# Interleaving the first-half depth of two batches at the start of a second layer, in two PSUM banks

## The chip, the cores and the metric

One core of a Trainium2 chip. The metric is the device time of one execution in microseconds (us); the median of several executions is quoted with the lowest and the highest. Where two kernels are compared, their executions alternate on the same chip. The spans of the profile are about 1.7 us shorter than the device time of the same execution.

An execution is labelled slow when it is over 1.5% above the fastest of the same kernel.

## The reference

A gated linear attention (four batches, eight heads of 48, sequence 768) is followed by a two-layer perceptron on its 3072 token vectors of 384:

```python
def _moe_ref(x, w_in, w_out):
    h = x @ w_in                          # 3072 x 384 by 384 x 2048
    g = h * (1.0 / (1.0 + np.exp(-h)))    # Silu
    return (g @ w_out)                    # by 2048 x 384
```

The attention runs over the sequence in six chunks of 128 tokens; the perceptron runs over the same chunks, four batches of 128 tokens each.

## The kernel before

The order of the program is the order on each engine. The perceptron's matmuls are "fillers": small closures in a list, which `fill(n)` emits between the steps of the attention, so that TensorE (PE) always has something to do. One part of the second layer is four matmuls of 128x128 by 128x384; a batch of a chunk takes four parts (sixteen depth tiles `ft`), all summed in one PSUM bank.

```python
opss = {}

def l2(sc, b, part):                      # second layer, chunk sc, batch b
    if part == 0:
        opss[0] = ps.tile([128, HD], FP, name="ops", tag="moe", bufs=3)
    ops = opss[0]
    for ft in range(4 * part, 4 * part + 4):
        nc.tensor.matmul(ops, gts[sc][:, ft, b * C:(b + 1) * C], wout[:, ft, :],
                         start=(ft == 0), stop=(ft == NFT - 1))
    if part == 3:
        osb = wrk.tile([128, HD], FP, name="osb", bufs=4)
        nc.vector.tensor_copy(out=osb, in_=ops)
        tt = b * S + sc * C
        nc.sync.dma_start(out=out[tt:tt + C, :], in_=osb)

def l2s(sc, b0=0, b1=B):
    return [(1.0, lambda b=b, part=part: l2(sc, b, part))
            for b in range(b0, b1) for part in range(4)]
```

The three banks of the ring "moe" are shared by these accumulators and by the first layer's tiles (`hps`), which ScalarE (ACT) empties through Silu. VectorE (DVE) copies the finished accumulators out (`osb`).

The second layer's weights come in two halves through GpSimd's (POOL's) own queue, depth tiles 0 to 7 and 8 to 15:

```python
def wout_part(g):
    nc.gpsimd.dma_start(
        out=wout[:, 8 * g:8 * g + 8, :],
        in_=moe_w_out[1024 * g:1024 * g + 1024, :].rearrange("(f p) n -> p f n", p=128))
```

They are issued between elementwise operations of POOL, and the second layer of chunk 0 begins soon after (short lines joined, cuts marked):

```python
wout_part(0)
sums(1); state(1)
...
wout_part(1)
fill(1)
sums(a); state(a)
...                                       # units 5 and 6 of the attention start
fillers.extend(l1s(1, 0, 2) + l2s(0))     # then chunk 0's second layer
sums(b_); state(b_)
fill(.5)
half_state(0); half_state(2)
front(B + 2)                              # POOL: ku, rku_f, kc of unit 6
```

## Time and profile before

| | |
|---|---|
| time, median of the first three executions | 197.36 us (197.13 to 197.82) |
| span of the profiled execution, which took 196.87 us | 195.2 us |
| PE busy | 97% |
| first matmul of the second layer | 46.60 us |
| ninth, the first that needs the second weight half | 49.54 us |
| second weight half issued / landed | 37.13 us / about 48.9 us |

A line of a timeline has the start in us, the duration, the engine, the line of the program, the operation, what it writes and reads, the shape and the count of merged instructions; brackets tell idle time just before it and what ended it. A line of busy time by stretch has the window, its length, then the busy time of PE, PE's weight loads, DVE, ACT and POOL, with the number of instructions of each, and last the granted PE clock, the DMA share and GB/s.

### The profile page before, as it was taken

How to read it: one execution, taken by the hardware profiler on the slowest of the kernel's cores; microseconds unless marked ns; L12 is line 12 of the kernel's file. 1: busy time of each engine (PE TensorE's matmuls, PEld its weight loads, DVE VectorE, ACT ScalarE, POOL GpSimd, SP SyncE). 2: the span in 40 equal slices, each digit the busy share in tenths (PEclk: the TensorE clock that was granted, in tenths of full speed). 3: DMA queues.
4: the chain of work that ended last, by engine and by line, in shares of the span. 5: the costliest groups of instructions: out<-in, count | busy, mean ns of one | idle time of the engine just before them, and what ended most of it. 6: DMA issues, size and time to landing. Idle time of an engine off the chain costs nothing.

```text
span 195.2 us, 4922 instructions
## 1 busy us (share of the span) xinstructions
PE 188.3 (97%) x1916; PEld 126.5 (65%) x1916; DVE 115.6 (59%) x233; ACT 91.0 (47%) x207; POOL 115.1 (59%) x145
## 2 busy tenths in 40 slices
PE   7989999899999999999999999999999999999993
PEld 2757778788667787665657656557656556644563
DVE  6985757884866775885477677457566344210121
ACT  3385587798212543226771025692026680069300
POOL 4679979989975779669668837844537710000000
PEclk9999999999999999999999999999999999999999
DMA  4999999999894674385646486615651011310022
GB/s 77 225 196 153 187 233 191 162 187 194 170 230 124 142 172 100 105 183 112 124 96 121 119 182 146 141 34 118 142 140 44 20 22 44 99 43 0 3 82 81
DMA packets 89696, 24.12 MB, mean 124 GB/s; under 512 B 82888, under 2 KB 89672, under 8 KB 89672
## 3 DMA queue, kind: packets, MB, share of 16 engines
q1 hardware_dynamic: 85980, 20.65, 48.9%
q0 software_dynamic: 3680, 3.15, 11.0%
q8 instruction: 15, 0.25, 0.5%
q14 instruction: 9, 0.07, 0.1%
q10 hardware_dynamic: 12, 0.00, 0.0%
HBM read 20.45 MB, written 4.72 MB: 129 GB/s over the span
## 4 chain that ended last, share of the span: by engine, by line
PE 80%; POOL 11%; DVE 2%; DMA 2%; issue 2%; SPq 1%; ACT 0%; POOLq 0%
PE ops L374 31%; PE hps L362 27%; PE ae L271 10%; PE xs L246 4%; POOL kc L197 3%; POOL rku_f L192 2%; POOL ku L186 2%; DMA kin<-in_k_dram 2%; PE y L297 2%; POOL vu L209 2%; PE y L294 2%; PE sps L313 1%; PE ops L388 1%; DVE am L280 1%; POOL win L417 1%
## 5 line engine op out<-in xcount | busy, mean ns | idle before, releaser
L365 ACT ACTIVATE gT<-hps 128x256 f16<-128x256 f32 (+1 forms) x128 | 59.7, 493 | 51.2 <-PE hps L362 49.5
L362 PE MATMUL hps<-xT,win 128*128 128x256 f16 (+1 forms) x384 | 69.2, 326 | 0.2
L374 PE MATMUL ops<-wout,gT 128*128 128x384 f16 x368 | 63.8, 326 | 0.0
L362 PEld LDWEIGHTS <-win 128*128 128x128 f16 x384 | 35.3, 98 | 23.2 <-issue 0.8
L374 PEld LDWEIGHTS <-gT 128*128 128x128 f16 x368 | 34.7, 98 | 22.4
L280 DVE TENSOR_TENSOR am<-ae,maskM 128x512 f16<-128x512 f32 x24 | 16.6, 692 | 30.6 <-PE ao L273 30.6
L378 DVE COPY osb<-ops 128x384 f32<-128x384 f32 x23 | 12.8, 555 | 28.8 <-PE ops L374 28.7
L209 POOL TENSOR_TENSOR vu<-vin,rku 128x384 f32<-128x384 f32 x23 | 19.0, 828 | 15.2 <-DVE rku L203 15.1
L271 PEld LDWEIGHTS ae<-rk 48*128 48x128 f32 x192 | 23.1, 187 | 7.4 <-issue 4.8
L271 PE MATMUL ae<-rk 48*128 48x128 f32 x192 | 27.6, 285 | 0.2 <-DVE rk L234 0.2
L273 PE MATMUL ao<-rk 48*128 48x128 f32 x192 | 27.6, 285 | 0.0
L186 POOL TENSOR_TENSOR ku<-kin,u_bc 128x384 f32<-128x384 f32 x24 | 24.1, 1006 | 5.0 <-ACT u_bc L153 3.6
L263 ACT CAST rT<-rk 112x512 f16<-112x512 f32 x20 | 12.3, 615 | 30.9 <-DVE rk L257 30.9
L257 DVE TENSOR_TENSOR rk<-xs,pif 112x512 f32<-112x512 f32 x40 | 25.6, 682 | 1.7 <-PE xs L246 1.7
L192 POOL TENSOR_TENSOR rku_f<-rin,ku 128x384 f32<-128x384 f32 x24 | 24.1, 1005 | 1.9
L197 POOL TENSOR_TENSOR kc<-kin,lamC 128x384 f16<-128x384 f32 x24 | 24.0, 1001 | 0.0
L273 PEld LDWEIGHTS ao<-rk 48*128 48x128 f32 x192 | 23.1, 187 | 0.0
L304 DVE TENSOR_TENSOR y<-y,vu 128x384 f16<-128x384 f32 x24 | 13.4, 557 | 8.9 <-POOL vu L209 3.6
L327 POOL CAST stb<-st 112x384 f16<-112x384 f32 x12 | 6.0, 503 | 20.7 <-DVE st L322 20.7
L280 DVE TENSOR_TENSOR am<-ao,maskM 128x512 f16<-128x512 f32 x24 | 16.4, 681 | 0.0
L203 DVE TENSOR_REDUCE rku<-rku_f 128x8 f32<-128x384 f32 x24 | 13.2, 550 | 2.4 <-POOL rku_f L192 2.0
L329 POOL TENSOR_TENSOR sdec<-st,pif 112x384 f32<-112x384 f32 x16 | 13.3, 835 | 0.9 <-ACT gT L365 0.8
(72 smaller groups left out, 167.1 us busy)
## 6 DMA issues: line engine op xcount, KB each, us to landing
rin<-in_r_dram SPq DMA_DIRECT2D x24, 192.0 KB, 2.9
kin<-in_k_dram SPq DMA_DIRECT2D x24, 192.0 KB, 3.5
vin<-in_v_dram SPq DMA_DIRECT2D x24, 192.0 KB, 3.6
out_dram<-osb SPq DMA_DIRECT2D x23, 192.0 KB, 1.9
win<-in_moe_w_in_dram POOLq DMA_DIRECT2D x4, 384.0 KB, 6.2
wout<-in_moe_w_out_dram POOLq DMA_DIRECT2D x2, 768.0 KB, 10.8
xT<-y SPq DMA_TRANSPOSE x18, 2.3
out_dram<-osh SPq DMA_DIRECT2D x1, 128.0 KB, 1.7
```

What stands on the lines that cost most here:

```text
L186: nc.gpsimd.tensor_tensor(out=L["ku"], in0=kin[i % NIN][:, :, 0:D], in1=u_bc, op=ALU.mult)
L192: nc.gpsimd.tensor_tensor(out=L["rku_f"], in0=rin[i % NIN][:, :, 0:D], in1=L["ku"], op=ALU.mult)
L197: nc.gpsimd.tensor_tensor(out=kc[i % NKC][:, :, 0:D], in0=kin[n][:, :, 0:D], in1=lamC, op=ALU.mult)
L209: nc.gpsimd.tensor_tensor(out=L["vu"], in0=vin[i % NIN], in1=L["rku"].unsqueeze(2).broadcast_to([128, H, D]), op=ALU.mult)
L257: nc.vector.tensor_tensor(out=rk[:, :, :, 64 * g:64 * g + 64], in0=xs[g][0:PR], in1=lam(g), op=ALU.mult)
L271: nc.tensor.matmul(ae[:, p, :], L["kT"][0:D, p, :], L["rT"][0:D, p, :], start=True, stop=True)
L273: nc.tensor.matmul(ao[:, p, :], L["kT"][64:PR, p, :], L["rT"][64:PR, p, :], start=True, stop=True)
L280: nc.vector.tensor_tensor(out=am, in0=a, in1=maskM.unsqueeze(1).broadcast_to([128, NP, C]), op=ALU.mult)
L304: nc.vector.tensor_tensor(out=L["y16"], in0=L["y"], in1=L["vu"], op=ALU.add)
L362: nc.tensor.matmul(hps, win[:, q, ft * 128:(ft + 1) * 128], xts[sc][:, q, b0:b1, :].rearrange("p b t -> p (b t)"), start=(q == 0), stop=(q ...
L365: nc.scalar.activation(out=gts[sc][:, ft, b0 * C:b1 * C], in_=hps, func=AF.Silu)
L374: nc.tensor.matmul(ops, gts[sc][:, ft, b * C:(b + 1) * C], wout[:, ft, :], start=(ft == 0), stop=(ft == NFT - 1))
```

## The change

The intent: begin the second layer with work that needs only the first half of the weights. The accumulator is now kept per batch, and the list of parts of chunk 0 is reordered, so that two batches run their first eight depth tiles before either needs the other half.

```diff
     def l2(sc, b, part):
         if part == 0:
-            opss[0] = ps.tile([128, HD], FP, name="ops", tag="moe", bufs=3)
-        ops = opss[0]
+            opss[b] = ps.tile([128, HD], FP, name="ops", tag="moe", bufs=3)
+        ops = opss[b]
...
-    fillers.extend(l1s(1, 0, 2) + l2s(0))
+    f = l2s(0)
+    fillers.extend(l1s(1, 0, 2) + f[0:2] + f[4:6] + f[2:4] + f[6:])
```

## The prediction

> **What bounds the kernel now.** I read the page first: its table of busy time, the strip of forty slices, and the chain of work that ended last.
>
> ```profile
> PE 188.3 (97%) x1916; PEld 126.5 (65%) x1916; DVE 115.6 (59%) x233; ACT 91.0 (47%) x207; POOL 115.1 (59%) x145
> PE   7989999899999999999999999999999999999993
> PE 80%; POOL 11%; DVE 2%; DMA 2%; issue 2%; SPq 1%; ACT 0%; POOLq 0%
> ```
>
> TensorE (PE) is busy for 97% of the span and carries 80% of the chain. The other engines appear in the chain early: listed in order of time, it is PE work almost without a break from about 38.8 us to 192.2 us, with nothing but PE from 46.76 to 61.57 us. The change lies in exactly that stretch: it reorders the start of chunk 0's second layer (the "ops" matmuls, L374), which begins at 46.6 us.
>
> The intent is easy to see from the code. The second-layer weight is loaded in two halves by GpSimd's queue (L421), depth tiles 0 to 7 and then 8 to 15. Before, batch 0 runs through all sixteen tiles at once, so its ninth matmul needs the second half. After, the first eight tiles of batch 1 come in between. The change therefore helps only if that ninth matmul waits for the transfer. I looked for such a wait in three views. First the PE timeline, with start, duration and group:
>
> ```profile
> 46.60 1.46 PE L374 MATMUL ops<-wout,gT 128*128 128x384 f16 x8
> ...
> 49.21 0.39 PE L246 MATMUL xs<-ident,kin 64*112 64x64 f32 x8
> 49.54 2.12 PE L374 MATMUL ops<-wout,gT 128*128 128x384 f16 x12
> ...
> 52.05 3.41 PE L374 MATMUL ops<-wout,gT 128*128 128x384 f16 x20
> ...
> 56.61 0.40 PE L246 MATMUL xs<-ident,kin 64*112 64x64 f32 x8
> 56.94 2.12 PE L374 MATMUL ops<-wout,gT 128*128 128x384 f16 x12
> ```
>
> The ninth matmul is the first of the x12 group at 49.54 us. It follows the kin transposes at 49.21 by 0.33 us. One unit later the same pair stands at 56.61 and 56.94, again 0.33 us apart, and there no transfer is in question. So the ninth matmul started when its turn came. Because matmul ends are modelled in the page, this comparison of starts is better evidence than the busy share.
>
> Second, the busy time by stretch (window, its length, PE busy with count, then the other engines):
>
> ```profile
> 46.60:49.60 3.00, 3.00 (x43) 2.23 (x41) 1.55 (x4) 2.29 (x6) 2.92 (x4) 1.00 1.03 185
> 49.60:52.00 2.40, 2.40 (x28) 1.62 (x28) 2.40 (x5) 0.27 (x2) 2.32 (x4) 1.00 0.76 152
> 52.00:55.40 3.40, 3.40 (x27) 1.92 (x24) 2.42 (x6) 1.30 (x3) 2.36 (x3) 1.00 1.10 245
> 55.40:61.40 6.00, 6.00 (x73) 4.38 (x73) 4.12 (x8) 0.62 (x1) 4.26 (x6) 1.00 0.71 169
> ```
>
> PE's busy time equals the length of every stretch; its clock is 1.00. There is no hole to close. Third, the transfer itself: queue q0 carries these weights, and its share of the DMA engines in the half microsecond up to 48.5 us and the next one is
>
> ```profile
> q0 software_dynamic: 20, 0.01, 16.1%
> q0 software_dynamic: 1, 0.00, 0.1%
> ```
>
> Its last packet falls just after 48.5 us. The second transfer was issued at 37.13 us and took 11.8 us to land: 37.13 + 11.8 = about 48.9 us. The ninth matmul starts at 49.54, so the data were there 0.6 us early.
>
> **What the Trainium skill says.** "TensorE: Matmul & The Clock Gate", Part 2, the step-by-step, says that only weight loads are pulled ahead and that the matmuls "stay in program order". A late weight half would hold all PE work behind it, and giving PE another batch to do first is the right cure. The 0.33 us pitch agrees that nothing was held here. "DMA: Bandwidth & Descriptors", on why a DMA increments its semaphore by 16, says that only the full count means that all data has landed; so it is the last packet that counts, and I took the landing at 48.9 us, not the bulk of the packets before 47.5. "PSUM — Partial Sum Buffer", the four PSUM rules, says that two accumulation groups open at once in the same bank and quadrant cannot both begin with the flag that starts a group. That is why the two batches need two banks, and the change gives them that; the trace of before, where one group is open at a time, cannot show it.
>
> **The change part by part.** It adds and removes no arithmetic: all 64 second-layer matmuls of chunk 0, each 128x384, remain, and the instruction order on PE, read from the compiled programs, has the same 2586 rows. Only the accumulator and depth tiles of the groups change.
>
> The second layer runs in parts of four matmuls, named here by batch and part. Before: 0-0, 0-1, 0-2, 0-3, 1-0, 1-1, 1-2, 1-3. After: 0-0, 0-1, 1-0, 1-1, 0-2, 0-3, 1-2, 1-3. A part takes 4 x 0.1625 = 0.65 us, since the chain has eight ops matmuls in 1.30 us (46.76 to 48.06). The first need for the second weight half moves back by two parts, 1.30 us, from 49.54 to about 50.84 us. Slack grows from 0.6 to about 1.9 us. **Worth on the path in this profile: 0.** If an execution has the transfer later by d, the gain is max(0, min(d - 0.6, 1.3)) us; at most 1.3 us or 0.66% of 197.36.
>
> The new costs, each against its slack:
> - Batch 1's accumulator is opened two parts sooner, at 49.54 instead of 50.84 us. It takes the bank of the fifth of the six first-layer tiles just before, whose Silu is in a pair that runs on ScalarE (ACT) from 47.35 for 0.66 us. Free by 48.0: no wait.
> - Batch 0's accumulator closes later. Part 0-3 is the first 0.65 us of the x20 group, so it ends about 52.8 us. Batch 3 next needs that bank at about 58.3 us. The order on VectorE (DVE) changes with it: the copy of batch 0, before at 51.59 us, comes after y and state, as the compiled order shows. DVE lines before:
>
> ```profile
> 51.59 0.55 DVE L378 COPY osb<-ops 128x384 f32<-128x384 f32 x1
> 52.15 0.56 DVE L304 TENSOR_TENSOR y<-y,vu 128x384 f16<-128x384 f32 x1
> 52.62 0.73 DVE L322 TENSOR_TENSOR st<-sps,sdec 48x192 f32<-48x192 f32 x2
> 54.20 0.56 DVE L378 COPY osb<-ops 128x384 f32<-128x384 f32 x1 [0.85 <-PE ops L374]
> ```
>
> y can start perhaps 0.1 us earlier, the state ends near 53.25, batch 0's copy runs 53.3 to 53.85, in the 0.85 us hole, and batch 1's copy stays at 54.20. Batch 0's bank is thus free 4.4 us early. Cost 0.
> - On the SP queue the store of batch 0 precedes the transpose of y and three loads. The store moves from 52.43 to about 53.9 us, the transpose from 53.20 to about 54.6, so landing (2.3 us, DMA issue list) near 57. The first-layer matmuls that read this half of xT start at 61.41 us. Cost 0. The loads move by the same 1.4 us, and feed a unit several 7 us units away.
>
> Sum: 0 removed, 0 added, and -0.2 us that I allow for executions in which the weights come late: the profiled run took 196.87 us and the three timed ones 197.13 to 197.82, so a late transfer may be among the causes of that spread, though nothing shows it.
>
> **The rivals.** (1) The wait is real in timed executions and hidden in the profiled one. For: the slack is only 0.6 us of an 11.8 us transfer, which shares the engines with q1. Against: the spread of the times is under 0.7 us. It would give 196.1 to 197.0 us. (2) A new wait: two accumulators held at once out of three rotating banks starve the first layer, or DVE's later copy delays y. For: the ring has three banks. Against: no first-layer tile is opened between 46.6 and 61.4 us, and the slacks above are 1.5 us and more. It would give 198 us. (3) The delayed SP queue collides with later loads or the transpose, and PE waits once. Against: 4 us of slack. If one wait of 1 us arose, 198.4 us.
>
> **Range and chances.** The main course is 197.36 - 0.2 = 197.2 us. Low end 196.5: most of rival 1. High end 197.9: the top of the times before. Two per cent is 3.9 us, three times the most that the reorder could save and more than any of the rivals costs. So faster 0.01, same 0.98, slower 0.01.
>
> **What would show it.** In the changed kernel's profile the x8, x12 and x20 groups should start at the same times relative to each other; the matmul that follows the kin transposes by 0.33 us should now write batch 1's accumulator; two osb copies should stand back to back on DVE behind the state; the transpose of y should issue 1.4 us later; PE's busy time in these stretches should still fill them. The prediction would be wrong if the time fell by over 0.7 us (timed runs hide a wait), or if a wait for Silu, an osb copy or xT appeared ahead of a matmul.

## The result and the profile after

| kernel | median us | range | executions |
|---|---|---|---|
| before | 197.36 | 197.13 to 197.82 | 6 |
| changed | 197.28 | 196.81 to 197.73 | 6 |

The ratio is 0.9993 with a 95% interval of 0.9974 to 1.0013: the same. Ratios here are the mean time of one kernel's fast executions over that of the other's from the same rounds, so not quite the ratio of the medians quoted beside them.

The page of the changed kernel, its busy times, the strip of PE and the shares of the chain that ended last:

```profile
PE 189.3 (97%) x1916; PEld 127.5 (65%) x1916; DVE 115.7 (59%) x233; ACT 91.0 (46%) x207; POOL 115.0 (59%) x145
PE   7989999899999999999999999999999999999993
PE 82%; POOL 9%; DVE 5%; issue 2%; ACT 0%; POOLq 0%; DVEq 0%
```

PE is as full as before. Its timeline, for the groups that the prediction showed:

```profile
47.45 1.46 PE L374 MATMUL ops<-wout,gT 128*128 128x384 f16 x8
...
50.06 0.39 PE L246 MATMUL xs<-ident,kin 64*112 64x64 f32 x8
50.39 2.12 PE L374 MATMUL ops<-wout,gT 128*128 128x384 f16 x12
...
52.90 3.41 PE L374 MATMUL ops<-wout,gT 128*128 128x384 f16 x20
...
57.47 0.39 PE L246 MATMUL xs<-ident,kin 64*112 64x64 f32 x8
57.79 2.12 PE L374 MATMUL ops<-wout,gT 128*128 128x384 f16 x12
```

Count each start from the first matmul of the second layer. Before, the groups came 2.94, 5.45 and 10.34 us after it (49.54, 52.05 and 56.94 less 46.60). After, they come 2.94, 5.45 and 10.34 us after it (50.39, 52.90 and 57.79 less 47.45). The reordered matmuls keep the same pace to the hundredth of a us. From that first matmul to the end of the span it is 195.2 - 46.60 = 148.60 us before and 196.0 - 47.45 = 148.55 us after (spans are given to 0.1 us). Two of the stretches, moved by the 0.85 us, show PE without a hole and at full clock, as before:

```profile
47.45:50.45 3.00, 3.00 (x43) 2.22 (x41) 1.55 (x4) 1.80 (x5) 2.92 (x4) 1.00 0.99 181
50.45:52.85 2.40, 2.40 (x28) 1.62 (x28) 2.07 (x4) 0.75 (x2) 2.32 (x4) 1.00 0.70 142
```

The 0.85 us by which this profiled execution is behind arises long before the change. The first group of first-layer matmuls already starts at 16.40 us, 0.84 us later than the 15.56 us of before. The PE timeline shows two filler matmuls and the group after them, first in the kernel before:

```profile
4.76 0.60 PE L127 MATMUL spin<-junk 128*128 128x512 f16 x2
5.20 0.55 PE L151 MATMUL rows<-ident,cols_sb 112*128 112x112 f32 x4
```

and the same in the changed kernel:

```profile
4.84 1.03 PE L127 MATMUL spin<-junk 128*128 128x512 f16 x2
5.66 0.95 PE L151 MATMUL rows<-ident,cols_sb 112*128 112x112 f32 x4
```

Here the fillers took 1.03 us instead of 0.60 us and the group after them 0.95 us instead of 0.55 us, and the next group started at 6.41 us instead of 5.58 us. These instructions are the same in both kernels. Three later profiles (t_now, the changed kernel again, and t_late below) start their first layer at 15.83, 16.01 and 15.64 us; so this is spread between executions. It also means that 197.73 us, the slowest of the changed kernel's six executions, owes its excess to its start and not to a wait for the weights.

What did move is DVE's order. Its timeline after:

```profile
53.00 0.56 DVE L304 TENSOR_TENSOR y<-y,vu 128x384 f16<-128x384 f32 x1 [0.48 <-PE y L297]
53.48 0.73 DVE L322 TENSOR_TENSOR st<-sps,sdec 48x192 f32<-48x192 f32 x2
54.24 0.56 DVE L378 COPY osb<-ops 128x384 f32<-128x384 f32 x1
55.05 0.56 DVE L378 COPY osb<-ops 128x384 f32<-128x384 f32 x1 [0.26 <-PE ops L374]
```

Batch 0's copy now stands behind y and the state, in a hole that was there. The SP queue's timeline, with the store of batch 0 and the transpose of y, before:

```profile
52.43 0.68 SPq L380 DMA_DIRECT2D out_dram<-osb  x1
53.20 1.22 SPq L344 DMA_TRANSPOSE xT<-y  x1
```

and after:

```profile
54.83 0.36 SPq L380 DMA_DIRECT2D out_dram<-osb  x1
55.24 1.21 SPq L344 DMA_TRANSPOSE xT<-y  x1
```

Counted from the first second-layer matmul the transpose went from 6.60 to 7.79 us, 1.19 us later, and nothing on PE waited for it.

### The profile page after: what moved, and what is told of

Same layout as the page of the kernel before. It is cut to its first block, busy times and chain, and to the rows that moved or that the text cites. A ratio compares the mean times of both kernels' runs of the same rounds, so it can differ in the third digit from the quotient of the medians.

```text
span 196.0 us, 4920 instructions
## 1 busy us (share of the span) xinstructions
PE 189.3 (97%) x1916; PEld 127.5 (65%) x1916; DVE 115.7 (59%) x233; ACT 91.0 (46%) x207; POOL 115.0 (59%) x145
## 4 chain that ended last, share of the span: by engine, by line
PE 82%; POOL 9%; DVE 5%; issue 2%; ACT 0%; POOLq 0%; DVEq 0%
PE ops L374 31%; PE hps L362 27%; PE ae L271 10%; PE xs L246 4%; POOL kc L197 2%; PE spin L127 2%; PE y L297 2%; POOL ku L186 2%; DVE am L280 2%; PE y L294 2%; POOL rku_f L192 2%; POOL vu L209 1%; PE sps L313 1%; PE ops L388 1%; POOL win L417 1%
## 5 line engine op out<-in xcount | busy, mean ns | idle before, releaser
L365 ACT ACTIVATE gT<-hps 128x256 f16<-128x256 f32 (+1 forms) x128 | 59.7, 493 | 51.0 <-PE hps L362 49.3
```

What stands on the lines that cost most here:

```text
L365: nc.scalar.activation(out=gts[sc][:, ft, b0 * C:b1 * C], in_=hps, func=AF.Silu)
```

## The experiments

The theory: in the kernel before, no matmul waits for the second weight half, so the reorder has nothing to remove; it buys 1.30 us of tolerance per two parts moved. The rivals: the timed executions hide a wait which the profiled one does not show; or the reorder has a gain that is eaten by a cost in banks, copies or the queue. If the theory holds, a transfer made late on purpose must make the kernel before wait and the changed one wait less.

In a sentence on the names: "b" is the order before, "a" the changed order, "t" an order in which three batches come first.

### The weights late by several us

In three kernels the second half is issued after POOL's elementwise work for unit 6, the third unit of chunk 1:

```diff
-    wout_part(1)
...
     front(B + 2)
+    wout_part(1)
```

Kernel b_late is the order before with this edit.

> The kernel before, with the second half of the second-layer weights issued later on GpSimd: after the elementwise work for unit 6, at about 44.4 us instead of 37.1 us. Estimate of the landing: the second transfer before lay behind the first in the same queue (first landed at 43.5, second at 48.9, so 5.4 us of moving), and the first needed about 2 us from issue to its first packets; so 44.4 + 2.2 + 5.5 = about 52.1 us. My theory (nothing waited in before, slack 0.6 us; the reorder is worth whatever the transfer is later than that, up to 1.3 us): PE now stands about 52.1 - 49.5 = 2.6 us ahead of the ninth ops matmul, and the time is 197.4 + 2.6 = about 200.0 us (199.0 to 201.0). Rival (timed runs of before already waited for this half, by some tenths of a us): the time grows by the full delay of 3.2 us, to about 200.6 us. Rival (the transfer is hidden anyway and its place does not matter): 197.4 us.

Kernel a_late is the changed order with it.

> The changed kernel with the same later issue. My theory: the first need is two parts (1.30 us) later, so of the 2.6 us stall that the kernel before has, 1.3 us remain, ahead of the seventeenth ops matmul; time about 198.7 us, that is 1.3 us (0.65%) below b_late. Rival (two open accumulators or the moved copies cost something that hides the gain): difference to b_late under 0.7 us. Rival (the transfer's place does not matter): equal to b_late and to the kernel before.

Kernel t_late has it too, and takes the reorder one batch further, so that all three banks are open:

```diff
-    fillers.extend(l1s(1, 0, 2) + f[0:2] + f[4:6] + f[2:4] + f[6:])
+    fillers.extend(l1s(1, 0, 2) + f[0:2] + f[4:6] + f[8:10] + f[2:4] + f[6:8] + f[10:])
```

> The same later issue, and three batches run the first half of their depth before any runs the second, so all three banks of the ring are open at once. The first need then comes after six parts, at about 52.7 us in the profile of before, so a landing at 52.1 us leaves no stall: time about 197.3 us, 1.3 us below a_late. Rival (three open accumulators starve the ring): a new wait of PE for a copy by VectorE or a Silu, and a time above a_late's.

Six executions of each, with the kernel before beside them at 197.45 us (196.99 to 198.44, 11 executions):

| kernel | median us | range | executions at clock below 0.995 | ratio of fast executions to before |
|---|---|---|---|---|
| b_late | 202.21 | 199.25 to 204.87 | 4 of 6 | 1.0149 |
| a_late | 199.56 | 198.06 to 201.62 | 2 of 6 | 1.0069 |
| t_late | 197.13 | 196.86 to 198.74 | none of 6 | 0.9999 |

The executions of b_late were 203.84 (the profiled one), 202.41, 199.25, 204.87, 202.01 and 200.20 us, with mean clocks of 0.983, 0.991, 0.999, 0.983, 0.991 and 0.998. Those of a_late were 199.42 (profiled), 198.97, 198.06, 199.70, 201.62 and 201.21 us, with 1.000, 1.000, 0.999, 1.000, 0.991 and 0.991. So the profile of b_late is of an execution labelled slow, and what follows for its clock is read from that profile.

The PE timeline of b_late around its ninth second-layer matmul:

```profile
47.52 1.46 PE L374 MATMUL ops<-wout,gT 128*128 128x384 f16 x8
...
53.76 4.00 PE L374 MATMUL ops<-wout,gT 128*128 128x384 f16 x12 [3.23 <-DMA wout<-in_moe_w_out_dram]
...
58.52 3.89 PE L374 MATMUL ops<-wout,gT 128*128 128x384 f16 x20
...
63.88 2.12 PE L374 MATMUL ops<-wout,gT 128*128 128x384 f16 x12
```

and of a_late, where the twelve are split by the wait:

```profile
46.99 1.46 PE L374 MATMUL ops<-wout,gT 128*128 128x384 f16 x8
...
49.93 1.47 PE L374 MATMUL ops<-wout,gT 128*128 128x384 f16 x8
53.39 0.81 PE L374 MATMUL ops<-wout,gT 128*128 128x384 f16 x4 [1.99 <-DMA wout<-in_moe_w_out_dram]
```

and of t_late, where the group of twenty runs through:

```profile
52.36 3.41 PE L374 MATMUL ops<-wout,gT 128*128 128x384 f16 x20
```

This is the wait that the change is meant for. With the order before it is 3.23 us. With the changed order eight more matmuls go first and 1.99 us are left, 1.24 us less. These are two executions, so count again from the first second-layer matmul: the data came at 6.24 us in b_late (53.76 - 47.52) and at 6.40 us in a_late (53.39 - 46.99), and PE ran dry at 3.01 and at 4.41 us. The need moved by 1.40 us by these modelled ends, where the prediction's arithmetic from starts said 1.30. With three batches first no wait is left: in the profiled t_late the data landed at 44.65 + 7.3 = 51.95 us, and its first need is four matmuls into the group at 52.36, about 53.0 us. From its first second-layer matmul to the end of the span it is 195.5 - 46.91 = 148.59 us, as without the delay. Two of its six executions took 198.21 and 198.74 us; they have no profile, and the kernel before has two such of its eleven (198.26 and 198.44 us).

Two parts of the expectations missed. The landings, expected at 52.1 us, were at 53.75 us (45.25 + 8.5) in b_late and 53.3 us (44.73 + 8.6) in a_late, while t_late had 51.95 us: a spread of 1.8 us for one program position. And b_late, at 202.21 us above its expected range of 199.0 to 201.0, lost far more than its wait. Its busy times by stretch, from about the start of the wait (53.76 - 3.23 = 50.53 us) on:

```profile
50.50:53.70 3.20, 0.02 (x2) 0.05 (x1) 2.48 (x4) 0.62 (x1) 3.12 (x5) 0.84 1.29 154
53.70:56.20 2.50, 2.44 (x8) 1.13 (x8) 0.00 (x0) 0.00 (x0) 1.70 (x2) 0.50 1.08 210
56.20:58.20 2.00, 2.00 (x17) 1.23 (x16) 0.56 (x1) 0.00 (x0) 0.00 (x0) 0.50 0.11 40
```

The granted clock, third from the end, fell to 0.50 and stayed there after the wait; it reads 1.00 again from 59.5 us. The twelve matmuls took 4.00 us where they take 2.12. From the first second-layer matmul to the end of the span b_late has 202.1 - 47.52 = 154.58 us, 5.98 more than before's 148.60: 3.23 us of waiting and 2.75 us more. The lower clock accounts for these: from the twelve to the twenty it is 4.76 us instead of 2.51, and from the twenty to the next twelve 5.36 instead of 4.89, together 2.72 us. In a_late the same count is 197.7 - 46.99 = 150.71 us, 2.11 more, of which 1.99 is the wait; its clock stayed at 1.00 in the profiled execution. Between these two profiles lie 3.9 us, three times what the reorder saves in waiting; the rest is clock. The medians differ by 2.65 us. The changed order did not rule out the loss of clock: the two slowest executions of a_late, 201.21 and 201.62 us, had a mean clock of 0.991. That it made the loss less frequent (two of six against four of six) is not shown by so few executions. The ratios of fast executions understate the difference, since the label removes most of those that lost clock.

### The deeper reorder alone

Kernel t_now has three batches first, with the weights issued where they were.

> Three batches' first halves first, with the weights issued where they were. My theory: nothing waits in either order, so this is the same as before and after, 197.3 us (within 0.3 us), slack about 3.8 us. Rival (the timed runs hide a wait that the change removed in part): a further gain of some tenths. Rival (bank pressure): a loss of 0.5 us or more with a wait ahead of the fourth batch's first matmul.

197.38 us (197.00 to 197.74), ratio 0.9992 (0.9969 to 1.0016): the same. In its profile the second half landed at 37.92 + 12.0 = 49.92 us and the twelve began at 50.36 us. From the first second-layer matmul to the end of the span it is 196.0 - 47.42 = 148.58 us. Still more tolerance bought nothing either, and three open accumulators cost nothing.

### A shorter delay, and a flaw in the experiment

To find a delay that the change absorbs in full, the issue was placed earlier among POOL's operations of unit 6 (its old place stays empty, as in the late kernels):

```diff
-    front(B + 2)
+    nat_v(B + 2)
+    nat_ku(B + 2)
+    wout_part(1)
+    nat_rk(B + 2)
+    nat_kc(B + 2)
```

> The kernel before, with the second weight half issued after GpSimd's first operation for unit 6, at about 42.3 us (in the late kernels it was issued at 44.7 to 45.3 us and landed 7.3 to 9.0 us after, where the profile shows it). Estimate of the landing: 42.5 + 8.5 = about 51 us. My theory: PE stands about 51.0 - 49.6 = 1.4 us ahead of the ninth ops matmul (0.5 to 2), once; a wait this short does not lower the clock of the matmuls after it, so the time is 197.4 + 1.4 = 198.8 us. Rival (every wait costs more than its length, as in b_late, where a stall of 3.2 us went with 4.8 us of time): 199.5 us or more, with the twelve matmuls after the wait at a pitch over 0.17 us.

> The changed kernel with this same issue. My theory: its first need is at about 50.9 us plus the start's shift, so at most 0.3 us of the wait remains and mostly none; time about 197.4 us, 1.3 us below b_mid: this is the delay at which the change pays in full. Rival (the reorder has a cost of its own that no wait had shown): over 198 us with no wait for the weights in the profile.

b_mid took 199.19 us (197.81 to 200.19), a_mid 198.40 us (197.65 to 199.05), before beside them 197.48 us; the ratios to before are 1.0084 and 1.0041. a_mid has no wait for the weights in its profile, and yet its median was 0.9 us above the kernel before: as the rival had it. (The profile is of its fastest execution, 197.65 us.) The waits of PE in b_mid around this place show one reason:

```profile
PE sps L313 <- POOL kc L197: 0.7, 1, 0.7
PE ops L374 <- DMA wout<-in_moe_w_out_dram: 0.7, 1, 0.7
```

The first line is in a_mid's answer as well, the second is not. An issue takes POOL 0.94 us, and here that stood ahead of kc, which the state's matmuls need. The edit had put a new wait into both kernels. So kc was moved ahead of the issue:

```diff
-    front(B + 2)
+    nat_v(B + 2)
+    nat_kc(B + 2)
+    wout_part(1)
+    nat_ku(B + 2)
+    nat_rk(B + 2)
```

> As b_mid, but without its flaw: there the issue of the weights stood ahead of the kc operation of unit 6, which the state's matmuls need, and PE waited 0.7 us for it in both kernels. Here kc goes first, then the issue, then ku and rku_f. Issue expected at about 42.3 us, landing 8.5 to 8.8 us later, about 51.0 us. My theory: no wait of PE for kc; one wait of about 1 us (0.5 to 1.7) ahead of the ninth ops matmul; no lower clock after it; time about 198.4 us (198.0 to 199.2). Rival (a wait of any length costs clock): 199.3 us or more.

> The changed kernel with the same issue. My theory: the wait is gone altogether or down to 0.3 us, and the time is that of the kernels with early weights, 197.4 us (197.0 to 197.8), about 1 us below b_mid2. Rival (a_mid's 0.9 us over the kernel before was not the kc wait but a cost of the reorder that shows only with late weights): about 198.3 us again.

b_mid2 took 199.50 us (198.35 to 199.86), a_mid2 198.52 us (197.22 to 199.44), before beside them 197.26 us (196.89 to 197.78). They were run on another chip. The wait for kc is gone from both, as expected. The PE timeline of b_mid2:

```profile
51.72 2.11 PE L374 MATMUL ops<-wout,gT 128*128 128x384 f16 x12 [1.80 <-DMA wout<-in_moe_w_out_dram]
```

and of a_mid2:

```profile
53.40 0.81 PE L374 MATMUL ops<-wout,gT 128*128 128x384 f16 x4 [2.28 <-DMA wout<-in_moe_w_out_dram]
```

Both expectations missed. b_mid2's median lies above its range of 198.0 to 199.2 us, where its rival had put it (199.3 us or more, since any wait costs clock); but the clock that this rival needs did not fall, all six executions have a mean of 1.000. a_mid2's profiled execution waited 2.28 us, longer than b_mid2's. The issues were at the same place (42.68 and 42.48 us), but the data landed after 9.0 us in one and after 10.9 us in the other. The profiled execution was one of a_mid2's two slowest, 199.43 us; its fastest took 197.22 us, which is the time of a kernel that waits for nothing. So the median difference, 0.98 us (ratios to before 1.0099 and 1.0046), agrees with a gain of up to 1.3 us per execution, over landings that differ by 1.9 us between these two profiles. With these two profiles alone one would have concluded that the change makes the wait longer. No wait of 1.80 or 2.28 us lowered the clock: it reads 1.00 in both, and the twelve matmuls of b_mid2 took 2.11 us. Without a loss of clock a wait costs its length: from the first second-layer matmul to the end of the span it is 197.3 - 46.91 = 150.39 us in b_mid2 and 197.7 - 46.71 = 150.99 us in a_mid2, 1.79 and 2.39 us above 148.60, for waits of 1.80 and 2.28 us. So the wait for kc was a flaw of b_mid and a_mid; that a_mid's 0.9 us is wholly that wait is not shown, since landings in the executions without a profile are not known.

### A bank fewer

```diff
-... tag="moe", bufs=3)
+... tag="moe", bufs=2)
```

in all three places, for the order before (b_ring2) and the changed one (a_ring2).

> The kernel before with two instead of three banks in the ring that first-layer tiles and second-layer accumulators share. Expected slower, since each first-layer tile's matmuls (0.65 us, or 0.33 us at half width) must then wait for the Silu of the tile two earlier (0.49 us mean, on average): somewhere from 198 to 205 us. It is the base line for the next one.

> The changed kernel with two banks: both are then held by the two open accumulators. My theory: in this stretch batch 2's accumulator is opened at about 54.2 us (profile of before), 0.3 us after batch 0's copy is done (estimate 53.9 us), and no first-layer tile is opened, so even with two banks the reorder costs nothing or one short wait: within 0.3 us of b_ring2. Rival (two open accumulators need the third bank): a wait of PE ahead of the ops matmuls for a copy by VectorE, and a time 0.5 us or more above b_ring2.

b_ring2 took 207.43 us (207.08 to 208.05, 6 executions), a_ring2 207.94 us (207.83 to 208.06, 4 executions): ratios to before 1.0500 and 1.0527, whose intervals overlap (1.0472 to 1.0528, 1.0499 to 1.0554). Between the times this stays open. The two profiles, which took 207.94 and 207.83 us, show no difference on PE. Its busy time from 48 to 70 us in b_ring2:

```profile
48.00:70.00 22.00, 20.53 (x222) 14.43 (x222) 14.34 (x28) 7.35 (x19) 16.35 (x19) 1.00 0.75 161
```

and in a_ring2:

```profile
48.00:70.00 22.00, 20.53 (x223) 14.44 (x222) 14.44 (x28) 7.35 (x19) 16.35 (x19) 1.00 0.74 162
```

The waits of PE in this window are the same two in both, 0.7 us for a Silu and 0.3 us for a copy ahead of a first-layer tile. From the first second-layer matmul to the end of the span both have 155.70 us (206.2 - 50.50 and 206.1 - 50.40). The third bank is worth 10 us to this kernel, but not for the sake of the two open accumulators.

### The changed kernel again

> The changed kernel as it is, again, with five rounds on a chip where the kernel before runs beside it: to see whether a hidden wait of some tenths of a us was in the timed runs of before. My theory: same within 0.2%, 197.3 to 197.6 us, with the time from the start of the second layer to the end of the span at 148.6 us as in both profiles. Rival (hidden wait in some timed runs): before's median above this one's by 0.4 us or more.

196.97 us (196.83 to 197.47), before beside it 197.26 us: ratio 0.9985 with an interval of 0.9968 to 1.0002. They were run on another chip. From the first second-layer matmul to the end of the span it is 195.6 - 47.07 = 148.53 us. Here the second half landed at 37.70 + 11.6 = 49.3 us, and the twelve started at 50.01 us. The difference of the medians is 0.29 us and the interval includes no difference; a hidden wait in some executions of the kernel before is not excluded at this size.

## Why the prediction was right

The prediction gives 2586 rows of PE instructions as read from the compiled programs; the profiles count 1916 matmuls in both kernels.

**The bound.** Right. PE was and is full from 46 us on, and the time from the second layer's start to the end of the span is 148.60, 148.55, 148.58 and 148.53 us in the profiles of before, the change, t_now and the change again.

**No wait to remove.** Right, and shown from two sides: the starts of the groups did not move against each other by 0.01 us, and the late kernels show what a real wait looks like there: a PE line with the weights named as its releaser, and a time to the end of the span that is longer by that wait. The slack that was read as 0.6 us is confirmed by three more profiles with the issue in its old place (the change, t_now, the change again): the landing was 0.8, 0.4 and 0.7 us ahead of the start of the ninth matmul, where the order before would need it (50.39 - 49.6, 50.36 - 49.92, 50.01 - 49.3).

**The worth of the reorder, max(0, min(d - 0.6, 1.3)).** Its bound of 1.3 us agrees with the profiles of b_late and a_late: 3.23 against 1.99 us of waiting, 1.24 us less, and a need that moved by 1.40 us. What the formula lacks is the clock: the wait of 3.23 us cost b_late another 2.75 us.

**The allowance of 0.2 us for late transfers.** Neither shown nor refuted; that the forecast of 197.2 us came within 0.1 us of 197.28 is well inside the spread and no support for it. The medians differ by 0.08 us in the first rounds and by 0.29 us in the later ones, the intervals include a ratio of 1, and t_now, which tolerates most, has 0.9992. The spread between executions, which the prediction brought forward in its support, has at least one other source that was seen: 0.84 us of difference before 17 us of the span, where the change cannot act. Against its first rival the prediction set a spread under 0.7 us; in the later rounds the kernel before ran from 196.99 to 198.44 us, so that argument did not hold.

**The new costs.** All hidden, as worked out. The copy of batch 0 was expected to start at 53.3 us on the old scale and came at 54.24 - 0.85 = 53.39; that of batch 1 was to stay at 54.20 and came at 55.05 - 0.85 = 54.20. The one small miss is y, which was to start perhaps 0.1 us earlier and did not (53.00 - 0.85 = 52.15): it waits for its own matmuls. The transpose came 1.19 us later instead of 1.4.

**The rivals.** The second, banks or copies, is refuted for this stretch by the identical pace of t_now with three open accumulators, and with two banks by the profiles. The third, a late SP queue, did not show: no PE wait for xT. The first remains possible within the interval above. It was not tested where it would show: the only profile of the kernel before is of an execution of 196.87 us, faster than all six timed beside the change, and none of its slower executions was profiled.

## What to carry to other kernels

Before reordering work ahead of a transfer, look for the wait in the timeline of the engine that would gain: if the starts have the same pitch as at a place where no transfer is in question, the reorder is insurance, not speed. Such insurance was free here, and it can pay more than the waiting it saves where a wait would otherwise lower PE's clock, as the 3.23 us of b_late did. When delaying something on purpose, check that the delaying instruction does not stand ahead of something else that is needed, and do not judge from one profile when the delay itself varies.

## What the Trainium skill lacked or had wrong

- "TensorE: Matmul & The Clock Gate", Part 1, HAM oscillation, gives the rule of no PE gaps over about 3.4 us. In b_late a gap of 3.23 us was enough: the clock was at 0.50 in the stretches after it, and its mean of 0.84 over 50.50 to 53.70 us means (an estimate) that it fell about 1 us before the gap ended, some 2.1 us after PE ran dry. Gaps of 1.80, 1.99 and 2.28 us left it at 1.00, so length alone does not decide. The page's closing table warns of gaps over about 3 us, with which this gap agrees.
- The same page, "What's actually happening", says that the point where the matmuls get fast varies by about 0.5 us either way. Here the long durations (1.03 us for two fillers that can take 0.60) ended at about 4.8 us in the kernel before and at about 7.2 us in the changed one, with PE's first filler at 2.94 us in both, and the first layer then started 0.84 us later. That this is the page's warm-up is not shown: the clock column of the profile reads 1.00 in both.
- No page read for this case gives the variation of a landing between executions. With the issue of a 768 KB weight load at the same place, it was 9.0 and 10.9 us (b_mid2, a_mid2), and 8.5, 8.6 and 7.3 us for three kernels with a later place; at the old place four profiles (before, the change, t_now, the change again) have 11.6 to 12.0 us.
- "DMA: Bandwidth & Descriptors", "Issuing engines are not separate DMA queues", calls the time to initiate a DMA usually small relative to the DMA. For this load it was 0.94 us of GpSimd against landings of 7.3 to 12.0 us, so that holds; what the section lacks is that even so the issue can be on the path of a computing engine: put ahead of an operation that PE needed, it cost PE 0.7 us (b_mid, a_mid).
